# One PSUM bank per projection, 128-wide transposes, a 512-wide half of the down projection, row turns inside gate and up, and fewer waits in a decode block

## The chip, the cores and the metric

The kernel runs on one core of one Trainium2 chip. The metric is the device time of one execution in microseconds (us), lower is better. Before the change the median of three runs is 440.13 us (439.95 to 440.18).

Five engines of the core work side by side and meet only through semaphores: TensorE (PE, matrix products and transposes, writing to the accumulation memory PSUM), VectorE (DVE), ScalarE (ACT), GpSimd (POOL) and SyncE (SP, which here only issues DMAs). Sixteen DMA engines move data between the large memory and the on-chip memory (SBUF).

## The reference

One decoding step of a transformer block for 8 sequences with one new token each: a modulation computed from a condition vector, grouped-query attention over a cache of 8192 positions (32 query heads, 4 key/value heads, head size 128), and a gated feed-forward network with a ReLU gate.

```python
mod = (_silu(c) @ w_mod).reshape(8, 6, 1, -1)            # c: 8 x 1024, w_mod: 1024 x 6144
sa, ca, ga, sb, cb, gb = (mod[:, i] for i in range(6))
h = _layernorm(x) * (1 + ca) + sa                         # x: 8 x 1 x 1024
q = h @ wq                                                # wq: 1024 x 4096, 32 heads of 128
scores = einsum(q, k) * Dh ** -0.5                        # k: 8 x 4 x 8192 x 128
o = einsum(softmax(scores), v) @ wo                       # wo: 4096 x 1024
x = x + ga * o
h = _layernorm(x) * (1 + cb) + sb
gate, up = h @ W_gate, h @ W_up                           # 1024 x 3584 each
x = x + gb * ((relu(gate) * up) @ W_down)                 # W_down: 3584 x 1024
```

Everything is bfloat16; the two caches hold 134 MB, the weights 51 MB. Each byte is read once.

## The kernel before, in words

**The stream.** All large inputs go through one SBUF buffer, `ring`, of five slots of 4 MB (`A_` to `E_`). `stream` lists the loads in the order in which SP issues them: wq in two halves, w_mod in two halves, the key block of the first pair, and then key block n+1 and value block n in turn; the two halves of wo; gate, up, gate, up in halves; W_down as `wd` 0 to 4 (half of it, a quarter, and the last quarter in pieces of four, two and one seventh). A pair n (of 16) is one sequence with two of its four key/value heads: 4 MB of keys, 4 MB of values. Each load waits until the last PE instruction that read the slot's former content is done, so SP's queue is held back by PE alone (L697 to L703).

**The graph.** `_Graph` records operations per engine with the operations that each depends on. `number` gives each engine a counting semaphore and `waits` turns dependencies into waits, leaving out those that the same engine has already waited for. The 16 pairs are emitted as a loop over two pairs (`emit`, L123 to L166): the instructions of the body are stored once and run eight times, and a wait inside it costs a register addition ahead of it.

**Head.** c and x are loaded as rows (8 x 1024), silu is applied to c, and both are turned to columns by PE transposes. `layernorm(xT)` is prepared. When a half of w_mod lands, 48 products of 8 columns of `siluT` with 512 columns of w_mod go to three PSUM banks: output j lies in bank j, in four strips of 32 partitions of which 8 are used. Three copies, twelve f32 transposes and three more copies give `modT`. wq is handled in the same way in two banks. `to_rows` turns the last modulation (gb) to rows, in 32 small f32 products.

**Pairs.** A pair takes 16 steps j (L609 to L647). In each, `slot_keys` transposes 1024 key vectors on PE (8 transposes of 128x128 into one of three PSUM banks), and DVE (even j) or ACT (odd j) copies the bank to `KT`. `slot_scores` multiplies them with the query. Amid the steps of pair n stands the softmax of pair n-1: maximum (`soft_max` to `soft_nb`, j = 2 to 5), exponentials and their sums on ACT (`soft_exp`, j = 6, 128 partitions x 1024), turning P to columns (`turn_p`, j = 8: 32 transposes of 64x64 into two banks, then two copies on DVE and two on ACT), and the product with the values (`pv`, j = 9 to 15). `early` puts the waits of `turn_p` on the last key transpose ahead of it.

**Tail.** `wo_part`, residual and `layernorm(x1T)`, `to_rows` of x1, then gate and up (128 products), ReLU and product, seven transposes to `hmT`, and the down projection: 112 products of 256 columns into bank `W`, four strips of 32 partitions. Two DVE operations add the residual and four small DMAs write the output.

## Time and profile before

| what | value |
|---|---|
| time, median of three runs | 440.13 us |
| time of the profiled execution | 440.24 us |
| its span, first to last instruction | 438.2 us |
| bytes read | 185.63 MB, 424 GB/s over the span |
| busy: PE, weight loads, DVE, ACT, POOL | 306.2, 198.5, 176.8, 187.4, 11.2 us |
| instructions executed | 11766 |
| DMA queue q1 (the stream): packets, share of 16 engines | 6928, 98.4% |
| DMA queue q8 (instructions): packets, MB | 10, 0.16 |
| last weights land, output DMAs issued | 434.5, 435.9 us |

Times in views of the trace are microseconds from the start of the span; the 2.0 us by which the execution is longer than its span lie outside it. Busy times can overlap, so a large one alone says nothing about what the time hangs on; the chain of waits and the tables by stage do.

### The profile page before, as it was taken

How to read it: one execution, taken by the hardware profiler on the slowest of the kernel's cores; microseconds unless marked ns; L12 is line 12 of the kernel's file. 1: busy time of each engine (PE TensorE's matmuls, PEld its weight loads, DVE VectorE, ACT ScalarE, POOL GpSimd, SP SyncE). 2: the span in 40 equal slices, each digit the busy share in tenths (PEclk: the TensorE clock that was granted, in tenths of full speed). 3: DMA queues.
4: the chain of work that ended last, by engine and by line, in shares of the span. 5: the costliest groups of instructions: out<-in, count | busy, mean ns of one | idle time of the engine just before them, and what ended most of it. 6: DMA issues, size and time to landing. Idle time of an engine off the chain costs nothing.

```text
span 438.2 us, 11766 instructions
## 1 busy us (share of the span) xinstructions
PE 306.2 (70%) x4987; PEld 198.5 (45%) x4987; DVE 176.8 (40%) x377; ACT 187.4 (43%) x214; POOL 11.2 (3%) x49
## 2 busy tenths in 40 slices
PE   0104267989888888788887878878888878565053
PEld 0101035656555655555555555555555655331031
DVE  4200046456363554535364444536355455330010
ACT  3000015566654746564574646547465655300000
POOL 4000000000000000000000000000000000000000
PEclk9999599999999999998999989999899999965586
DMA  8999999999999999999999999999999999999994
GB/s 350 446 449 449 413 432 424 428 432 427 431 431 431 431 431 434 434 431 434 434 434 440 440 437 434 431 434 434 431 431 431 431 431 431 436 436 420 428 428 181
DMA packets 7004, 185.83 MB, mean 424 GB/s; under 512 B 800, under 2 KB 832, under 8 KB 1104
## 3 DMA queue, kind: packets, MB, share of 16 engines
q1 hardware_dynamic: 6928, 185.61, 98.4%
q8 instruction: 10, 0.16, 0.1%
q10 hardware_dynamic: 64, 0.04, 0.0%
q14 instruction: 2, 0.02, 0.0%
HBM read 185.63 MB, written 0.02 MB: 424 GB/s over the span
## 4 chain that ended last, share of the span: by engine, by line
DMA 59%; PE 26%; DVE 6%; issue 5%; ACT 2%; SPq 1%; DVEq 0%; ACTq 0%
DMA ring<-in_A_k_cache_dram 34%; PE PS L374 14%; PE PS L370 12%; DMA ring<-in_w_mod_dram 11%; DMA ring<-in_B_W_down_dram 7%; DMA ring<-in_B_W_up_dram 7%; DVE KT L378 3%; ACT KT L381 2%; DVE tm L378 1%; SPq L700 1%; DVE nm L378 1%; ACT P L381 0%; DVE nb L378 0%; DVE qT L378 0%; DVE rl L378 0%
## 5 line engine op out<-in xcount | busy, mean ns | idle before, releaser
L381 ACT ACTIVATE KT<-PS 128x1024 bf16<-128x1024 bf16 (+1 forms) x132 | 132.8, 1008 | 164.5 <-PE PS L374 79.9
L374 PE MATMUL PS<-identb,ring 128*128 128x128 bf16 x2048 | 159.8, 223 | 34.7 <-DMA ring<-in_A_k_cache_dram 21.3
L378 DVE COPY KT<-PS 128x1024 bf16<-128x1024 bf16 (+1 forms) x130 | 89.6, 690 | 178.3 <-PE PS L374 117.9
L374 PEld LDWEIGHTS PS<-identb,ring 128*128 128x128 bf16 x2048 | 120.5, 100 | 79.4 <-issue 46.2
L370 PE MATMUL PS<-KT,Z 128*32 128x512 bf16 x516 | 54.3, 396 | 0.2 <-ACT KT L381 0.2
L370 PE MATMUL PS<-ring,pt 128*32 128x256 bf16 x1088 | 50.0, 275 | 0.8 <-DVE pt L378 0.8
L370 PE MATMUL PS<-ring,siluT 128*8 128x512 bf16 x96 | 9.6, 576 | 31.5 <-DMA ring<-in_w_mod_dram 31.5
L370 PEld LDWEIGHTS PS<-ring,pt 128*32 128x32 bf16 x1088 | 23.0, 95 | 13.2 <-issue 0.9
L381 ACT ACTIVATE pt<-PS 64x512 bf16<-64x512 bf16 x34 | 20.1, 591 | 16.7 <-PE PS L374 16.3
L381 ACT ACT_TABLE_LOAD x11 | 14.1, 1283 | 24.0 <-PE PS L374 22.3
L370 PE MATMUL PS<-ring,h2T 128*8 128x512 bf16 (+1 forms) x128 | 11.2, 519 | 15.9 <-DMA ring<-in_B_W_up_dram 11.0
L381 ACT ACTIVATE P<-PS,nb 128x1024 bf16<-128x1024 f32 x17 | 18.9, 1113 | 6.5 <-DVE nb L378 5.6
L370 PEld LDWEIGHTS PS<-KT,Z 128*32 128x32 bf16 x516 | 13.8, 93 | 15.3 <-ACT KT L381 1.7
L378 DVE TENSOR_REDUCE mp<-PS 128x1 f32<-128x1024 f32 x17 | 20.7, 1215 | 0.0
L370 PEld LDWEIGHTS PS<-ring,siluT 128*8 128x8 bf16 x96 | 2.9, 115 | 37.9 <-DMA ring<-in_w_mod_dram 32.3
L378 DVE COPY pt<-PS 64x512 bf16<-64x512 bf16 x34 | 14.2, 417 | 2.7 <-PE PS L374 2.1
L370 PEld LDWEIGHTS PS<-ring,h2T 128*8 128x8 bf16 x128 | 3.6, 113 | 23.0 <-DMA ring<-in_B_W_up_dram 12.6
L370 PE MATMUL PS<-od,selo 128*128 128x128 f32 x36 | 9.8, 359 | 5.0 <-DVE od L378 5.0
L378 DVE TENSOR_TENSOR KT<-PS,KT 128x512 bf16<-128x512 f32 (+1 forms) x2 | 1.2, 619 | 26.4 <-ACT KT L381 26.4
L374 PE MATMUL PS<-identb,KT 8*128 8x8 bf16 (+1 forms) x31 | 2.5, 211 | 13.2 <-DMA KT<-in_A_x_dram 8.2
L374 PE MATMUL PS<-identb,P 64*64 64x64 bf16 x544 | 11.8, 194 | 0.0
L598 POOL CAST ot<-og 128x16 bf16<-128x16 f32 x16 | 4.1, 255 | 287.2 <-DVE og L378 287.2
(88 smaller groups left out, 158.4 us busy)
## 6 DMA issues: line engine op xcount, KB each, us to landing
ring<-in_A_k_cache_dram SPq DMA_DIRECT2D x16, 4096.0 KB, 21.1
ring<-in_A_v_cache_dram SPq DMA_DIRECT2D x16, 4096.0 KB, 30.0
ring<-in_w_mod_dram SPq DMA_DIRECT2D x2, 6144.0 KB, 42.4
ring<-in_A_wq_dram SPq DMA_DIRECT2D x2, 4096.0 KB, 16.8
ring<-in_A_wo_dram SPq DMA_DIRECT2D x2, 4096.0 KB, 29.4
ring<-in_B_W_gate_dram SPq DMA_DIRECT2D x2, 3584.0 KB, 26.7
ring<-in_B_W_up_dram SPq DMA_DIRECT2D x2, 3584.0 KB, 33.1
ring<-in_B_W_down_dram SPq DMA_DIRECT2D x1, 3584.0 KB, 39.5
```

Of the source, the lines that this page charges most:

```text
L370: return pe(lambda e: e.matmul(out_, lhsT, rhs, start=start, stop=stop, skip_group_check=True), reads, writes, block, deps)
L374: return pe(lambda e: e.matmul(out_, in_, ident, start=True, stop=True, is_transpose=True), reads, writes, block)
L378: return g.op("dve", lambda e: getattr(e, name)(*args, **kw), reads, writes)
L381: return g.op("act", lambda e: e.activation(*args, **kw), reads, writes)
L598: pool(lambda e: e.tensor_copy(dst, og[:, n % 2]), reads=[("og", n % 2)], writes=[("ot", n // B)])
L700: o.fn = (lambda e, key=key, src=src, o=o: e.dma_start(place[key], src).then_inc(o.sem, 16))
```

## The change

Seven edits are made together.

- *Fewer waits.* A new pass `thin` drops every dependency that is implied by another one that the operation, or an earlier one on its engine, already waits for. `early` and the field `apart` go.
- *c and x together.* Both are loaded into one tile of 16 rows and turned together by 8 transposes instead of 16; the sigmoid now waits for both.
- *One bank for w_mod and one for wq.* `siluT` is widened to 40 columns and `hT` to 24, with zeros beside the 8 that count. A product takes 24 (or 16) columns, so that output j falls 8j rows down in the strip and adds zeros to the others; all 96 (64) products accumulate in one bank. One copy and four transposes follow where there were three copies and twelve transposes (two and eight for wq).
- *P in blocks of 128.* `soft_exp` becomes two ACT instructions of 64 partitions each, writing the second half 64 columns further on in a `P` of 1088 columns; `turn_p` turns it with 8 transposes of 128x128 per half, 16 instead of 32.
- *`to_rows` with a wide operand.* DVE spreads the source into `wide` (128 x 8 x 128); 8 f32 products with `rest` replace 32. Constants `part`, `rest`, `fold` and a cleared `wide` are made at the start.
- *Its place.* Both calls now stand after k = 3 of gate and up, ahead of the products that wait for the second halves; one stood before the first key block, the other before gate and up.
- *Half of W_down in 512 columns.* The part of `wd` 0 takes 28 products of 512 columns into bank `Y`, a copy to `yR`, and two f32 products with `fold` that put the sum into `W`; the other half goes on in `W` as before.

The built programs hold 1205 PE products before and 1063 after; the program of PE has 2641 instructions before and 2262 after, counting the weight load of each product, and four for an f32 product that is no transpose.

```diff
--- before.py
+++ after.py
...
+    def thin(self):
+        place = {id(o): (eng, i) for eng, ops in self.prog.items() for i, o in enumerate(ops)}
+        name = lambda d: ("dma", id(d.sem)) if d.sem is not None else place[id(d)][0]
+        value = lambda d: d.semval if d.sem is not None else place[id(d)][1] + 1
...
+                    kept = set()
+                    for k, d in best.items():
+                        v = value(d)
+                        if base.get(k, 0) >= v:
+                            continue
+                        if any(known[id(x)].get(k, 0) >= v for y, x in best.items() if y != k):
+                            continue
+                        kept.add(k)
...
     def number(self):
+        self.thin()
...
-        siluT = sb("siluT", [128, KD, B], bf16)
+        siluT = sb("siluT", [128, KD, 5 * B], bf16)
-        hT = sb("hT", [128, KD, B], bf16)
+        hT = sb("hT", [128, KD, 3 * B], bf16)
-        P = sb("P", [128, 1024], bf16)
+        P = sb("P", [128, 1088], bf16)
...
+                        (Z[:], 0.0, ("Z", 0)), (siluT[:], 0.0, "siluT"), (hT[:], 0.0, "hT"), (pt[:], 0.0, "pt"), (od[:], 1.0, "od"), (P[:], 0.0, ("P", 0)), (KT[:, 6, :], 0.0, ("KT", 6)), (KT[:, 7, :], 0.0, ("KT", 7))):
...
+        dve("memset", wide[:], 0.0, writes=["wide"])
+        for i in range(2):
+            dve("tensor_reduce", fold[:, i].rearrange("p (h s r) -> p h s r", h=2, s=2)[:, :, i, :],
+                identf[:].rearrange("p (a h r) -> p h r a", a=2, h=2), AX.X, ALU.add, reads=["identf", "fold"], writes=["fold"])
...
+        g.dma("act", KT[B:2 * B, 0, :], c, csem, 16, writes=["c"])
+        g.dma("act", KT[0:B, 0, :], A_x.rearrange("b o d -> (b o) d"), xsem, 16, writes=["x"])
+        act(sig, row, ACT.Sigmoid, reads=["c", "x"], writes=[("KT", 1)])
...
+        for k in range(KD):
+            tr(TB(0)[:, 2 * B * k:2 * B * (k + 1)], sig[:, k::KD], identb[0:2 * B, 0:2 * B], [("KT", 1), "identb"], [pT[0]])
...
             for j in range(3):
                 for q in range(4):
-                    mm(bank(j)[32 * q:32 * q + B, :], siluT[:, k, :], fourths(w, 2 * j + q // 2, q % 2), k == 0, k == KD - 1,
-                       ["siluT"], [pB[j]], ("mod", k // 4))
+                    mm(bank(0)[32 * q:32 * q + 3 * B, :], siluT[:, k, (2 - j) * B:(5 - j) * B], fourths(w, 2 * j + q // 2, q % 2),
+                       k + j == 0, k == KD - 1 and j == 2, ["siluT"], [pB[0]], ("mod", k // 4))
+        dve("tensor_copy", modR, bank(0), reads=[pB[0]], writes=[("KT", 0)])
+        t = PS[:, 4, :]
+        for i in range(4):
+            tr(t[:, 128 * i:128 * (i + 1)], modR[:, i::4], identf[:], [("KT", 0), "identf"], [pT[0]])
         for j in range(3):
-            if j == 1:
...
-            t = PS[:, 4 + j, :]
-            for i in range(4):
-                tr(t[:, 128 * i:128 * (i + 1)], modR[j][:, i::4], identf[:], [("KT", j), "identf"], [pT[j]])
             dve("tensor_copy", modT[:, 2 * j:2 * j + 2].rearrange("p s (h i) b -> p i (s h) b", h=2),
-                t.rearrange("p (i q x) -> p i q x", i=4, q=4)[:, :, :, 0:B], reads=[pT[j]], writes=["modT"])
+                t.rearrange("p (i q x) -> p i q x", i=4, q=4)[:, :, :, B * j:B * (j + 1)], reads=[pT[0]], writes=["modT"])
...
-                mm(bank(j)[32 * q:32 * q + B, :], hT[:, k, :], w[:, 512 * f:512 * (f + 1)], k == 0, k == KD - 1,
-                   ["hT"], [pB[j]], ("wq", k // 4))
+                mm(bank(1)[32 * q:32 * q + 2 * B, :], hT[:, k, (1 - j) * B:(3 - j) * B], w[:, 512 * f:512 * (f + 1)],
+                   k + j == 0, k == KD - 1 and j == 1, ["hT"], [pB[1]], ("wq", k // 4))
+        dve("tensor_copy", qR, bank(1), reads=[pB[1]], writes=[("KT", 2)])
+        for i in range(4):
+            tr(TB(0)[:, 128 * i:128 * (i + 1)], qR[:, 128 * i:128 * (i + 1)], identb[:], [("KT", 2), "identb"], [pT[0]])
...
         def to_rows(dst, dkey, src, skey):
-            dve("memset", W[:, 0:256], 0.0, writes=[pW])
+            dve("tensor_tensor", out=wide.rearrange("p k (q x) -> p k q x", q=4)[:, :, :, 0:B], in0=src[:, :, None, :].to_broadcast([128, KD, 4, B]),
+                in1=part[:, None, :, None].to_broadcast([128, KD, 4, B]), op=ALU.mult, reads=[skey, "part"], writes=["wide"])
             for k in range(KD):
-                for q in range(4):
-                    mm(W[32 * q:32 * q + B, 32 * k:32 * (k + 1)], src[:, k, :], identf[:, 32 * q:32 * (q + 1)], True, True, [skey, "identf"], [pW])
+                mm(W[:, 32 * k:32 * (k + 1)], wide[:, k, :], rest[:], True, True, ["wide", "rest"], [pW])
             dve("tensor_copy", dst.rearrange("p (x k) -> p k x", k=8), W[:, 0:256].rearrange("p (k x) -> p k x", k=8), reads=[pW], writes=[dkey])
-
-        to_rows(gbR[:], "gbR", modT[:, 5], "modT")
...
         def soft_exp(n):
-            act(P[:], S(n).rearrange("p h c -> p (h c)"), ACT.Exp,
-                bias=nb[:], scale=SCALE, accum_out=od[:, 128:129], reads=[pS(n, 0), pS(n, 1), "nb"], writes=["P", "od1"])
-
+            for gl in range(2):
+                r = slice(64 * gl, 64 * (gl + 1))
+                act(P[r, 64 * gl:64 * gl + 1024], S(n)[r].rearrange("p h c -> p (h c)"), ACT.Exp,
+                    bias=nb[r], scale=SCALE, accum_out=od[r, 128:129], reads=[pS(n, 0), pS(n, 1), "nb"], writes=[("P", gl), ("od1", gl)])
         def turn_p(n, h):
             t = t_bank()
-            at = len(g.prog["pe"])
             for i in range(8):
-                for gl in range(2):
-                    r = slice(64 * gl, 64 * (gl + 1))
-                    tr(TB(t)[r, 64 * i:64 * (i + 1)], P[r, 512 * h + 64 * i:512 * h + 64 * (i + 1)], identb[r, r], ["P", "identb"], [pT[t]])
-            if n + 1 < NP:
-                early(at)
-
+                at = 64 * (8 * h + i)
+                tr(TB(t)[:, 128 * i:128 * (i + 1)], P[:, at:at + 128], identb[:], [("P", 0), ("P", 1), "identb"], [pT[t]])
...
-        modulate(h2T, "h2T", 3, 4)
-        to_rows(x1R[:], "x1R", x1T, "x1T")
+        modulate(h2T[:], "h2T", 3, 4)
...
+            if k == 3:
+                to_rows(gbR[:], "gbR", modT[:, 5], "modT")
+                to_rows(x1R[:], "x1R", x1T[:], "x1T")
...
-        for c_ in range(4):
+        for t in range(14):
+            w = place[("wd", 0)][:, t // 7, t % 7, :]
+            for h in range(2):
+                at = 64 * (t % 2) + 32 * h
+                mm(Y[at:at + B, :], hmT[:, t % 7, t // 7, :], w[:, 512 * h:512 * (h + 1)], t < 2, t >= 12, ["hmT"], [pY], ("wd", 0))
+        dve("tensor_copy", yR[:], Y, reads=[pY], writes=["yR"])
+        for i in range(2):
+            mm(W[:, 0:256], fold[:, i], yR[:, 256 * i:256 * (i + 1)], i == 0, False, ["yR", "fold"], [pW])
+        for c_ in (2, 3):
             for i in range(7):
-                if c_ < 2:
-                    key, w = ("wd", 0), place[("wd", 0)][:, c_, i, :]
-                elif c_ == 2:
+                if c_ == 2:
...
                 for q in range(4):
-                    mm(W[32 * q:32 * q + B, 0:256], hmT[:, i, c_, :], w[:, 256 * q:256 * (q + 1)], c_ + i == 0, c_ == 3 and i == 6,
+                    mm(W[32 * q:32 * q + B, 0:256], hmT[:, i, c_, :], w[:, 256 * q:256 * (q + 1)], False, c_ == 3 and i == 6,
                        ["hmT"], [pW], key)
```

## The prediction

> **What bounds the kernel now.** I read the page from the DMA row to the chain of waits, then the last microseconds in tables by stage, then one pair in order of time.

> ```profile
> DMA  8999999999999999999999999999999999999994
> GB/s 350 446 449 449 413 432 424 428 432 427 431 431 431 431 431 434 434 431 434 434 434 440 440 437 434 431 434 434 431 431 431 431 431 431 436 436 420 428 428 181
> ...
> q1 hardware_dynamic: 6928, 185.61, 98.4%
> q8 instruction: 10, 0.16, 0.1%
> ...
> DMA 59%; PE 26%; DVE 6%; issue 5%; ACT 2%; SPq 1%; DVEq 0%; ACTq 0%
> ```

> The sixteen DMA engines are never idle between the first and the last slice: the kernel is its stream. PE's 26% in the chain are the steps at which a slot comes free, and a load that is issued then stands behind others: the key load issued at 253.42 us lands at 275.60, 22 us for 4 MB that take 9.7 us at 432 GB/s. Nothing that PE, DVE or ACT do faster amid the stream can shorten it; only its start, its end, and what the DMA engines carry besides can.

> The end, in windows of 1 us; the last two columns are the DMA engines' share and GB/s:

> ```profile
> 430.00:431.00 1.00, 0.97 (x28) 0.59 (x28) 0.00 (x0) 0.00 (x0) 0.00 (x0) 0.85 0.94 369
> 431.00:432.00 1.00, 0.09 (x4) 0.00 (x0) 0.00 (x0) 0.00 (x0) 0.00 (x0) 0.50 0.63 254
> 432.00:433.00 1.00, 0.28 (x8) 0.21 (x12) 0.00 (x0) 0.00 (x0) 0.00 (x0) 0.50 0.30 119
> 433.00:434.00 1.00, 0.80 (x20) 0.23 (x16) 0.00 (x0) 0.00 (x0) 0.00 (x0) 0.50 0.13 51
> ```

> The share falls over three microseconds: the engines do not finish together, and the last two (0.13 of 16) decide when the weights are there. The chain ends on that:

> ```profile
> 405.17 28.73 DMA ring<-in_B_W_down_dram
> 433.90 0.04 issue
> 433.95 0.60 PE PS L370 x7
> 434.55 0.02 issue
> 434.56 0.41 PE PS L370 x4
> 434.98 0.02 issue
> 435.00 0.44 DVE ov L378
> ```

> **Why two engines are late.** The trace holds every DMA packet with queue, start, duration and size. On a busy engine a packet starts 3 to 4 ns before its predecessor ends, which separates the sixteen series; all carry the same sequence of sizes. Their last weight packets end so: six engines at 430.8 to 431.1 us; two, which took an 8 KB packet of another instruction queue (at 76.3 and 101.9), at 431.9; six, which took one 16 KB packet of q8, at 432.3 to 432.5; two, which took two of those, at 433.87 and 434.01. So one q8 packet sets its engine back by about 1.4 us (0.95 for itself, 0.45 for a slower packet after it; at 430.72 an 8 KB packet takes 787 ns instead of 309), and an engine that is never idle never makes it up.

> The ten come at 55.7, 70.4, 77.2, 85.8, 93.1, 100.5, 377.6, 387.4, 403.7 and 429.8 us: none in the last seven passes of the loop. 16 KB are 256 instructions of 64 bytes, and PE's program has 2641, so eleven blocks, ten after the first. Along PE's program each packet comes some 80 instructions ahead of a multiple of 256, 3 to 4.4 us late. The first eight hit eight different engines; the ninth hits that of the first, the tenth that of the second.

> [...]

> **The change, part by part.**

> *Head.* Three more memsets on POOL stand ahead of `identf` (by `pt`, 1.82 us for 2048 columns, some 1.4 us for their 1600), and DVE gets some 3 us of constants (four reductions of 0.2 to 0.4, a 1024-column clear bounded by the 0.53 of 512 columns twice). The sigmoid now waits for x, which lands at 8.16, not for c alone (2.98). Together siluT and the layer norm, ready at 12.8 and 16.3, come 5 to 8 us later; w_mod lands at 37.12. Cost 0; without that cover, up to 8 us.

> *w_mod and wq.* The same 96 and 64 products. Wider weights are bounded by 0.115 (8 columns) and 0.093 us (32 columns) a load, both beside the products; accumulating in one bank has no row: bounded below by 0 and above by doubling the second batch of 4.61 us. After it two copies, eight f32 transposes (0.14 each) and, for wq, four of bf16 fall away: about 0.6 us; `to_rows` of gb (1.2 us) goes. PE starts on the keys 1.5 to 2 us sooner than 67.28. This buys nothing: the keys of pair 0 have landed before, and key block 1, value block 0 and wo, issued at 56.62 and 63.36, keep the engines busy past 90. At the upper bound the first of them slips to 61.2, where the sixteen engines end the keys of pair 0 (60.3 to 61.9): up to 0.9 us of idle. I take 0, since the four strips that run side by side are as before.

> *Pairs.* From the pair at 275.60:

> ```profile
> 282.26 1.11 ACT L381 ACTIVATE P<-PS,nb 128x1024 bf16<-128x1024 f32 x1
> ...
> 283.37 1.01 ACT L381 ACTIVATE KT<-PS 128x1024 bf16<-128x1024 bf16 x1
> 284.43 0.10 PEld L374 LDWEIGHTS PS<-identb,ring 128*128 128x128 bf16 x1 [0.75 <-ACT KT L381]
> ...
> 284.60 0.69 PE L374 MATMUL PS<-identb,P 64*64 64x64 bf16 x32
> ...
> 292.16 0.33 SPq L700 DMA_DIRECT2D ring<-in_A_k_cache_dram  x1
> ```

> The second ACT half is unseen: bounds 0.59 (the 64x512 copy to `pt`) and 1.11 us (128x1024 exponential), plus 0.19 for the sum; I take 1.11 as the nearer in columns, so ACT +1.3. The j = 7 copy behind it on ACT, for whose bank the second half of `turn_p` waits, slips by as much. The first half starts at about 284.6, the second at 285.7, and both cost 8 x 128x128 (0.62, the key rows) where 32 small ones took 0.69. The next key step slips from 285.54 to 286.4, so the pair from 16.6 to some 17.7 us. What falls away in waits I count at nothing. The stream gives 19.4 us per pair (issues at 253.42, 274.15 and 292.16), so PE waits shorter for the next keys. Cost 0; bounds 0 and 15 times what a pair takes beyond 19.4.

> *Gate, up and the turns.* gate and up first halves wait for up at 399.04; h2T is ready at 393.43. The two `to_rows` now run from 403.7 on PE: 8 f32 products each, bounded by 0.25 us (the `pick` rows: 2.04 for four) and 0.5 us each, 4 to 8 us with two DVE copies of 0.63 and two spreads of 0.4 to 1.0. Behind them waits only the first gate product of the second half (landed 408.86), which in any case waits on with its followers for up at 417.33. Cost 0, and SP's next load waits for the last gate product ahead of them (404.05), unmoved.

> *Down.* 28 products of 512 columns for 56 of 256: wo's 32 of that form took 1.99 us, so 1.74 against 1.70. Then 0.69 for the copy and two f32 products of 256 columns, 1.0 to 1.9 us (128 columns: 0.5). `wd` 0 lands at 425.79, so `W` is ready at 429.3 to 430.2, and `wd` 1 lands at 430.03; its 1.06 us have until 432.72. Cost 0; without that cover up to 0.8 us, when the clock is at half, as it is in the last window.

> *Instruction blocks.* PE's program shrinks to 2262: 8.8 blocks, eight after the first. By the order above they hit eight different engines, and the last weight packet ends at 432.5 instead of 434.0: -1.5 us. The last four products (0.41), two DVE steps and the output DMAs follow as before. A block ahead of need for instruction 2304 would be asked for near 2224, among the products of `wd` 2, which PE can't pass before about 431.2; 3 us on, the stream is over.

> Sum: 440.24 (profiled execution) - 1.5 = 438.7 us. The median of the runs is 0.1 below that execution, which I leave in the range. 0.2% (0.9 us) is about what a measurement can tell from no change.

> **Rivals.** *No gain, 440.2.* Fetches may stop mattering for the end, or two of the eight may share an engine: the choice of engine is read from ten cases only. The slowest of the two late engines then ends where it did. For it speaks that the loop's five fetches cost PE nothing visible; against it, that lateness and packets match on all sixteen engines. [...]

> *Half a gain, 439.3 to 439.9.* A ninth block is asked for earlier, or the copy and `fold` run at the half clock and PE is 0.6 to 0.8 us behind the last load.

> *Slower, 443.* If the split exponential and the blocks of 128 make a pair longer than the stream's 19.4 us, PE falls behind in each. At the end 5.6 us (393.4 to 399.0) and 4.4 us (after the turns, to the last up block, near 416: 417.33 less the second hit of 403.7) are spare, 10 in all over 15 pairs: it decides from 20.0 us a pair, 3.4 more than now, where I find 1.1. At 20.3 the lag is 14 us, 4 beyond the spare: 440.2 - 1.5 + 4.2 = 442.9.

> **Numbers.** Forecast 0.62, no gain 0.18, half a gain 0.12 (split over the bound), slower 0.08. The forecast's own range is 438.2 to 439.1: ends of engines with one packet differ by 0.3, its delay by 0.3. The range runs from there to 440.4, past the case of no gain, and leaves out 0.1 above. Faster 0.69, same 0.22, slower 0.09.

> **What would show it.** q8 with 8 packets (9 with one after 433 us); the last weights at PE near 433.0 instead of 434.56; DMA rows at 9 throughout; the key loads still some 19.4 us apart; DVE waiting less for `wd`. Wrong: a last landing at 434.5 with eight q8 packets, an idle DMA engine amid the pairs, or PE busy when the last load lands.

## The result and the profile after

The kernel after takes 438.55 us (median of seven runs, 438.53 to 438.86) where the kernel before takes 440.13 (439.95 to 440.20) beside it: a ratio of 0.9966, 95% interval 0.9956 to 0.9976, so 1.58 us or 0.36% faster. The forecast was 438.7 with a range of 438.2 to 440.4. The profiled execution is one of 438.55 us with a span of 436.6.

The page of the kernel after, its DMA row, two of its queues and the shares of the chain of work that ended last:

```profile
DMA  8999999999999999999999999999999999999995
...
q1 hardware_dynamic: 6928, 185.61, 98.7%
q8 instruction: 9, 0.15, 0.1%
...
DMA 54%; PE 23%; issue 8%; DVE 8%; ACT 6%; SPq 1%; DVEq 0%; ACTq 0%
```

The stream carries the same 6928 packets and is as dense as before (9 in every slice between the first and the last), and the same bytes are done sooner. The end, first in windows of 1 us (columns: window, its length, busy time of PE, PEld, DVE, ACT and POOL, granted clock, DMA share, GB/s), then as the chain:

```profile
431.00:432.00 1.00, 0.61 (x16) 0.30 (x16) 0.00 (x0) 0.00 (x0) 0.00 (x0) 1.00 0.67 266
432.00:433.00 1.00, 0.40 (x10) 0.11 (x10) 0.00 (x0) 0.00 (x0) 0.00 (x0) 0.99 0.33 119
433.00:434.00 1.00, 0.38 (x4) 0.09 (x4) 0.54 (x2) 0.00 (x0) 0.00 (x0) 0.50 0.00 0
```

```profile
404.40 28.55 DMA ring<-in_B_W_down_dram
432.95 0.04 issue
433.00 0.41 PE PS L422 x3
433.41 0.02 issue
433.43 0.43 DVE ov L430
433.87 0.02 issue
433.89 0.42 DVE outR L430
```

Between 433 and 434 us the DMA share is 0.00, where it was 0.13 before: the two engines that came last are gone. The last weights reach PE at 433.00 instead of 434.56, and from there the same steps of 0.41, 0.43 and 0.42 us follow. The whole gain in the span (438.2 to 436.6) lies in that landing, and all the down weights show it: `wd` 0 is at PE at 424.50 (before 425.79), `wd` 1 at 428.73 (430.03), `wd` 2 at 431.16 (432.72).

The packets say why. Their times, here and in the prediction, count from 0.13 us after the start of the span, so they read 0.13 us lower than the views. The nine of q8 come at 55.6, 75.1, 84.8, 93.1, 102.7, 378.7, 388.5, 419.8 and 432.3 us. The first eight are on eight different DMA engines; the ninth starts within 5 ns of the end of its engine's last weights. Six engines end at 430.9 to 431.2, two with an 8 KB packet at 431.7 and 432.1, and eight with one 16 KB packet at 432.3 to 432.5. None ends later.

### The profile page after: what moved, and what is told of

Read it like the earlier page. It is cut to its first block, busy times and chain, and to the rows that moved or that the text cites. A ratio compares the mean times of both kernels' runs of the same rounds, so it can differ in the third digit from the quotient of the medians.

```text
span 436.6 us, 10734 instructions
## 1 busy us (share of the span) xinstructions
PE 306.9 (70%) x4575; PEld 199.4 (46%) x4575; DVE 180.0 (41%) x384; ACT 208.6 (48%) x246; POOL 12.7 (3%) x52
## 3 DMA queue, kind: packets, MB, share of 16 engines
q1 hardware_dynamic: 6928, 185.61, 98.7%
## 4 chain that ended last, share of the span: by engine, by line
DMA 54%; PE 23%; issue 8%; DVE 8%; ACT 6%; SPq 1%; DVEq 0%; ACTq 0%
DMA ring<-in_A_k_cache_dram 29%; PE PS L426 12%; DMA ring<-in_w_mod_dram 11%; PE PS L422 11%; DMA ring<-in_B_W_down_dram 7%; DMA ring<-in_B_W_up_dram 6%; ACT P L433 3%; DVE KT L430 2%; ACT KT L433 2%; DVE tm L430 1%; DVE ov L430 1%; DVE nm L430 1%; SPq L747 1%; DVE nb L430 0%; DVE rl L430 0%
## 5 line engine op out<-in xcount | busy, mean ns | idle before, releaser
L426 PE MATMUL PS<-identb,ring 128*128 128x128 bf16 x2048 | 152.8, 220 | 19.3 <-DMA ring<-in_A_k_cache_dram 17.6
L426 PEld LDWEIGHTS PS<-identb,ring 128*128 128x128 bf16 x2048 | 117.0, 98 | 58.5 <-issue 37.3
L422 PE MATMUL PS<-KT,Z 128*32 128x512 bf16 x516 | 51.9, 390 | 0.1
L433 ACT ACTIVATE P<-PS,nb 64x1024 bf16<-64x1024 f32 x34 | 37.7, 1109 | 6.2 <-DVE nb L430 4.2
L426 PE MATMUL PS<-identb,P 128*128 128x128 bf16 x272 | 21.0, 221 | 20.2 <-ACT P L433 14.5
L422 PEld LDWEIGHTS PS<-ring,pt 128*32 128x32 bf16 x1088 | 24.5, 95 | 12.8 <-issue 0.8
L422 PE MATMUL PS<-ring,siluT 128*24 128x512 bf16 x96 | 9.8, 584 | 27.5 <-DMA ring<-in_w_mod_dram 27.5
L426 PEld LDWEIGHTS PS<-identb,P 128*128 128x128 bf16 x272 | 15.3, 98 | 26.5 <-DVE KT L430 17.2
L433 ACT ACTIVATE pt<-PS 64x512 bf16<-64x512 bf16 x34 | 20.1, 592 | 13.5 <-PE PS L426 13.2
L430 DVE COPY pt<-PS 64x512 bf16<-64x512 bf16 x34 | 14.4, 422 | 17.7 <-PE PS L426 17.2
L422 PEld LDWEIGHTS PS<-ring,siluT 128*24 128x24 bf16 x96 | 3.1, 125 | 33.5 <-DMA ring<-in_w_mod_dram 28.3
L426 PE MATMUL PS<-identb,KT 128*128 128x128 bf16 (+1 forms) x19 | 1.7, 218 | 18.4 <-DVE KT L430 18.4
```

What stands on the lines that cost most here:

```text
L422: return pe(lambda e: e.matmul(out_, lhsT, rhs, start=start, stop=stop, skip_group_check=True), reads, writes, block, deps)
L426: return pe(lambda e: e.matmul(out_, in_, ident, start=True, stop=True, is_transpose=True), reads, writes, block)
L430: return g.op("dve", lambda e: getattr(e, name)(*args, **kw), reads, writes)
L433: return g.op("act", lambda e: e.activation(*args, **kw), reads, writes)
```

## The experiments

Four questions were open: whether it is the instruction packets, whether any other edit has a part in the gain, what order the packets follow, and how thin the cover is under which the longer pairs cost nothing.

### One block more in the kernel after

```diff
+        def filler(n):
+            for i in range(n):
+                q = 32 * (i % 4)
+                mm(PS[q:q + B, 5, 0:32], identf[:, 0:B], identf[:, q:q + 32], True, True, ["identf"], [pT[1]])
...
         layernorm(xT, "xT")
+        filler(64)
```

> The kernel after, with 64 small f32 products (four PE instructions each) that write to a bank that is overwritten later, put into the head just ahead of the first products with w_mod, where PE waits for w_mod anyway: PE's program grows from 2262 to 2518 instructions, one block of 256 more. Theory (instruction packets set a DMA engine back): the packets come one block earlier along the program, the ninth now near 414 us, amid the stream, on the engine that took the first; the tenth near the end, harmless. That engine's last weight packet ends near 433.9, time 440.0. Rival (the gain came from the other edits, fewer waits and shorter stages): 438.6, unchanged.

Measured: 440.12 us, ratio to before 1.0003 (0.9993 to 1.0012). Sixty-four tiny products in a stretch in which PE only waits (they run from 19.45 to 21.35 us, and the first products with w_mod wait for it until 38.46) give the whole gain back. One of the eleven executions took 442.31, the others 439.80 to 440.26; it was not traced. The page, and the chain's end:

```profile
q8 instruction: 10, 0.16, 0.1%
```

```profile
425.96 3.19 PE PS L422 x28
...
429.92 5.16 PE PS L422 x46
435.08 0.02 issue
435.10 0.43 DVE ov L430
```

The ninth packet comes at 419.7 and one engine now ends at 433.99 (its last eight packets stand 0.08 us apart from 433.43 on, alone); the others end by 432.84. `wd` 0 is at PE at 425.96 instead of 424.50. This execution also shows a forecast rival at work, PE at half clock (0.50 from 430 to 434): its products run from 425.96 with no break but the copy to `yR`, and end at 435.08, 0.1 us after those of the kernel before. By these rows the 9.1 us from `wd` 0's landing to the last product would have ended at 433.6 in the kernel after, 0.2 beyond what it did. So the half clock is worth 0.2 us there at most; the rest is the late landing.

### One and two blocks less in the kernel before

```diff
         def to_rows(dst, dkey, src, skey):
-            dve("memset", W[:, 0:256], 0.0, writes=[pW])
-            for k in range(KD):
...
+            dve("memset", dst, 0.0, writes=[dkey])
```

> The kernel before without the two turnings to rows: the rows of gb and of x1 are set to zero instead, so the residual and the gate of the second half are left out. PE's program goes from 2641 to 2387 instructions, one block less. Theory: nine packets; the ninth still comes amid the stream and hits the engine of the first, so one engine keeps two hits and the time stays near 440.0 to 440.1, though PE has 64 products less. Rival (each instruction or each product saved is worth its share of 1.6 us over 379 instructions): about 439.0.

```diff
-        for c_ in range(4):
+        for c_ in (2, 3):
```

> The kernel before without the two turnings to rows (their rows are zero) and without the products with the first half of W_down (its weights are loaded as before, but not multiplied): PE's program has 2275 instructions, two blocks fewer than before and 13 more than after. Theory: eight packets that matter, on eight different engines, so 438.6, as the kernel after, although none of its other edits is made. Rival (the gain comes from the shorter stages, the fewer waits or the new order): 440.1.

Measured: 440.08 us with one block less, ratio 0.9999 (0.9990 to 1.0008), and 438.88 with two, ratio 0.9973 (0.9963 to 0.9982). The page and chain of the first:

```profile
q8 instruction: 9, 0.15, 0.1%
```

```profile
404.85 29.07 DMA ring<-in_B_W_down_dram
433.91 0.04 issue
433.96 0.60 PE PS L370 x8
```

And the chain of the second:

```profile
404.92 27.49 DMA ring<-in_B_W_down_dram
432.41 0.04 issue
432.45 0.60 PE PS L370 x7
```

Both pages count nine q8 packets. In the first the ninth comes at 428.3, amid the stream, and one engine ends at 434.05. In the second it comes at 432.5, behind the stream, and the last engine ends at 432.58. A cut of 254 instructions, 64 products among them, is worth nothing while the ninth packet stays; moving that one packet behind the stream is worth 1.2 us. The second has none of the change's edits, and keeps four fifths of its gain. Of the 0.3 us by which it is behind the kernel after, 0.1 lies in the span (436.7 against 436.6) and 0.2 outside it.

### The pass that drops waits, alone

```diff
     def number(self):
+        self.thin()
```

> The kernel before with the pass that drops implied waits, and nothing else: 2636 PE instructions, ten blocks after the first as before. Theory: ten packets, two engines hit twice, 440.1. Rival (the waits and the register additions that they cost inside the loop slow the pairs or the issuing of loads): less than 440.1, down to 438.6 if they were the whole gain.

Measured: 440.25 us, ratio 1.0003 (0.9994 to 1.0012), with ten q8 packets and two engines ending last, at 433.85 and 433.92. The pass does nothing for the time by itself.

### One block less in the kernel after

```diff
-            for i in range(16):
+            for i in range(2 if gp == 0 else 16):
...
-        for k in range(KD):
+        for k in (0, 1, 2, 3, 7):
...
-        for t in range(14):
+        for t in (12, 13):
```

> The kernel after with 264 PE instructions less, one block: the two turnings to rows (rows zero), the gate and up products of k = 4, 5 and 6, the products with the first half of wo but for two of 16, and those with the first half of W_down but for two of 14 are left out; all weights are loaded as before. Theory: seven or eight packets that matter, each on an engine of its own, so that the last engine still has one hit: 438.55, nothing gained. Rival (each block less is worth 1.5 us): 437.0.

Measured: 438.74 us, ratio 0.9972 (0.9964 to 0.9981). Seven packets instead of nine, the last engine at 432.61 instead of 432.53, no gain. Eight of the eleven executions lie at 438.58 to 438.86, the others at 439.54 to 440.18; the profiled one, 439.54, has a span of 436.7, as in the kernel after. Together with the others:

| kernel | PE instructions | q8 packets ahead of the end | last weight packet ends, us | time, us |
|---|---|---|---|---|
| after, one block less | 1998 | 7 | 432.61 | 438.74 |
| after | 2262 | 8 | 432.53 | 438.55 |
| before, two blocks less | 2275 | 8 | 432.58 | 438.88 |
| before, one block less | 2387 | 9 | 434.05 | 440.08 |
| after, one block more | 2518 | 9 | 433.99 | 440.12 |
| before with `thin` | 2636 | 10 | 433.92 | 440.25 |
| before | 2641 | 10 | 434.01 | 440.13 |

It is a step between eight packets and nine, with nothing on either side of it. The engines follow the packets one by one: with seven, seven engines end between 432.2 and 432.9 and none later; with eight, eight and none; with nine, seven there and one near 434.0; with ten, six there and two near 434.0. The others have ended by 432.1 in all seven traces.

### Eight and nine blocks more

```diff
+        filler(128)
         for k in range(KD):
             tr(TB(0)[:, 2 * B * k:2 * B * (k + 1)], sig[:, k::KD], identb[0:2 * B, 0:2 * B], [("KT", 1), "identb"], [pT[0]])
...
         layernorm(xT, "xT")
+        filler(256)
...
         for k in range(KD):
+            if k == 4:
+                filler(128)
```

The second has 320 where this has 256.

> The kernel after with 512 of the same small products in three places of the head: 2048 PE instructions more, eight blocks. Theory: seventeen packets, sixteen of them in time to matter, so that each of the eight engines is hit twice and none three times, the last harmless: the end is again that of an engine with two hits, 440.0, the same as with one block more. Rival A (the cost is in the number of instructions that PE goes through, or in bytes): eight times what one block costs, about 449 to 450. Rival B (nothing to do with it): 438.6.

> The kernel after with 576 of the same small products: 2304 PE instructions more, nine blocks. Theory: seventeen packets in time to matter, so that one engine is hit three times and its last weight packet ends near 435.3: 441.4, a step of 1.4 above the run with eight blocks more. If the cost went by the number of instructions, the step between the two would be an eighth of what eight blocks cost; if packets don't matter, 438.6 for both.

Measured: 445.43 and 448.41 us, 5.4 and 7.0 more than expected. Neither theory holds, for a reason that the windows of the first show:

```profile
25.00:30.00 5.00, 1.89 (x128) 1.74 (x128) 0.00 (x0) 0.00 (x0) 0.00 (x0) 0.50 1.08 465
30.00:35.00 5.00, 0.00 (x0) 0.00 (x0) 0.00 (x0) 0.00 (x0) 0.00 (x0) 0.50 1.08 465
35.00:40.00 5.00, 1.89 (x128) 1.74 (x128) 0.00 (x0) 0.00 (x0) 0.00 (x0) 0.50 0.89 383
...
60.00:65.00 5.00, 3.87 (x46) 1.59 (x36) 0.09 (x1) 0.00 (x0) 0.00 (x0) 0.81 0.21 88
```

PE goes through one block (64 f32 products, counted here as 128 products and 128 weight loads) and then stands still until after the next packet has come (17.3 us between 20 and 45 us, up to 5.6 at a time); the packets are 5.7 to 8.5 us apart (12.4, 18.4, 25.6, 32.6, 40.0, 47.1, 55.6, 61.3). The products with w_mod come late, the slots come free late, and between 60 and 65 us the DMA engines are at 0.21: the stream has run dry. Summed over the packets, the sixteen engines carry no load of the stream for 4.9 us more than in the kernel after up to 430 us (0.5 of it are the eight more instruction packets, the rest is idle), and the packets of the stream themselves take 2.0 us more per engine (32 KB packets of up to 2.3 us instead of 1.21 around the dry stretch): 6.9 of the 7.4 us by which this profiled execution (445.94) is longer. For the other the same sum gives 6.6 and 2.3, 8.9 of 9.9.

If a stream that runs dry brings all engines level again, what was late before it no longer counts; no run shows that by itself. Both kernels have eight packets between the dry stretch and the end, and in both the last engine ends within half a microsecond of the next ones, as with one packet each; but in the second, four engines end at 442.1 to 442.5, a microsecond behind the other twelve, which is not explained. The question of the order of the engines was thus not put by these two runs.

### Four blocks more, where PE waits

```diff
         layernorm(xT, "xT")
+        filler(128)
...
+            if k == 4:
+                filler(64)
...
                 to_rows(x1R[:], "x1R", x1T[:], "x1T")
+                filler(64)
```

> The kernel after with 256 of the small f32 products, put where PE waits longest: 128 behind the layer norm of x, 64 between the halves of w_mod, 64 behind the turning to rows: 1024 PE instructions, four blocks more, spread so that the stream of loads should not run dry (with eight and nine blocks more in the head it stood idle for 4 to 6 us). Theory (each packet sets back the next of eight engines in turn): twelve packets matter, four engines have two hits, none three: 440.1, as with one block more. Rival (each block costs its 1.5 us wherever it lands): 438.55 + 4 x 1.57 = 444.8.

Measured: 440.19 us (median of 12), ratio 1.0005 (0.9996 to 1.0015), where a cost for each block would have given 444.8. Ten of the twelve executions lie at 439.97 to 440.41. The other two, the profiled one among them, took 442.2 and 442.6. In that one the stream was dry for 0.6 us more, and one engine ended 1.2 us after the next (436.26 and 435.03), which would fit a third packet on one engine. So the median shows that twelve packets cost no more than nine. On which engines they fell in those ten executions was not traced, and that the turn through eight engines is always kept is not shown.

### How much longer a pair may take

The forecast let a pair grow to 20.0 us before it would cost anything. Extra exponentials on ACT, written to a tile that nobody reads, lengthen it:

```diff
         def soft_exp(n):
+            for i in range(2):
+                r = slice(64 * (i % 2), 64 * (i % 2) + 64)
+                act(extra[r, :], S(n)[r].rearrange("p h c -> p (h c)"), ACT.Exp, bias=nb[r], scale=SCALE,
+                    reads=[pS(n, 0), pS(n, 1), "nb", ("extra", i % 2)], writes=[("extra", i % 2)])
```

> The kernel after with two more exponentials of 64 x 1024 per pair on ACT, written to a tile that nothing reads: 2.2 us more per pair ahead of the second half of the turn of P, so about 19.9 us per pair where PE doesn't wait for the stream. The forecast's slack (10 us over 15 pairs, from 20.0 us a pair) gives 438.6, at most 439.5. Rival (no slack behind the pairs, every pair beyond the stream's 19.4 us moves the end): 438.6 + 15 x 0.55 = about 447.

> The kernel after with three more exponentials of 64 x 1024 per pair on ACT, 3.3 us per pair, about 21.0 us per pair. The forecast's slack is used up: 438.6 + 15 x (21.0 - 19.4) - 10 = about 453. Rival (work on ACT and PE amid the pairs is hidden whatever it takes): 438.6. Rival (no slack): about 463.

Measured: 471.19 and 486.91 us. The pairs took 21.3 and 22.5 us (mean distance of the key loads' issues from 88.5 to 365.7 and from 87.4 to 380.1), more than the 2.2 and 3.3 us that were added to 17.7 (at a mean granted clock of 0.885 and 0.873, where the kernel after has 0.945), and the slack of 10 us isn't there. With the sum of idle and slower packets again: 20.3 and 10.5 us per engine in the first, 30.8 of its 31.0; 36.6 and 10.6 in the second, all of its 47.2. So the time is lost where the stream runs dry amid the pairs, and what PE has to spare behind them did not bring it back. Without slack, 438.6 + 15 x (pair - 19.36) gives 468.0 and 486.0; the profiled executions, from which the pairs are, took 469.5 and 485.7.

With one extra exponential (`range(1)`):

> The kernel after with one more exponential of 64 x 1024 per pair on ACT (1.1 us). With two and three more the PE-bound pairs took 21.3 and 22.5 us; with one they should take between 19.4 and 20.1. The forecast's slack of 10 us gives 438.6 up to 20.0 us a pair. Theory formed after the two slower kernels (no slack: the last loads wait for PE as well, so each pair beyond the stream's 19.36 us moves the end): 438.6 + 15 x (pair - 19.36), so 443.6 at 19.7 and 449.7 at 20.1.

Measured: 447.73 us (445.56 to 449.34), ratio 1.0173 (1.0152 to 1.0195). The profiled execution is the shortest, 445.56; its pairs take 19.95 us in the mean, so that the theory without slack gives 438.6 + 15 x 0.59 = 447.4, 1.9 too much for it, and the forecast's slack 438.6, 7.0 too little. Idle time (2.2) and slower packets (4.7) make up 6.9 of these 7.0 us. The pairs are not alike, though. Three in a row, from one key load's issue to the next:

```profile
264.38:284.56 20.18, 17.22 (x252) 11.51 (x252) 9.47 (x19) 14.05 (x16) 0.34 (x2) 0.92 1.00 430
284.56:303.29 18.73, 15.77 (x252) 10.79 (x252) 9.48 (x19) 12.77 (x15) 0.34 (x2) 1.00 0.98 402
303.29:323.26 19.97, 17.15 (x252) 11.64 (x252) 9.47 (x19) 14.05 (x16) 0.34 (x2) 0.91 0.99 425
```

The middle one, at full clock, is 18.73 us: 1.0 more than the 17.73 of the kernel after, and under the stream's 19.36. Eleven of the 13 pairs have the lower clock and take 20.0 to 20.3. Inside the last one, PE's operations (start, duration, and in brackets the idle time before them), then windows of 1 us:

```profile
311.47 0.62 PE L427 MATMUL PS<-identb,ring 128*128 128x128 bf16 x8
313.99 0.76 PE L427 MATMUL PS<-identb,P 128*128 128x128 bf16 x8 [1.90 <-ACT P L434]
314.96 1.03 PE L427 MATMUL PS<-identb,P 128*128 128x128 bf16 x8 [0.21 <-ACT KT L434]
315.79 1.06 PE L427 MATMUL PS<-identb,ring 128*128 128x128 bf16 x8
```

```profile
313.00:314.00 1.00, 0.01 (x1) 0.02 (x2) 0.00 (x0) 0.98 (x3) 0.00 (x0) 1.00 0.91 393
...
315.00:316.00 1.00, 1.00 (x10) 1.00 (x11) 0.63 (x2) 0.00 (x0) 0.00 (x0) 0.50 0.91 393
316.00:317.00 1.00, 1.00 (x12) 0.72 (x14) 0.00 (x0) 0.96 (x2) 0.00 (x0) 0.50 1.07 459
317.00:318.00 1.00, 1.00 (x17) 0.41 (x10) 0.00 (x0) 0.97 (x2) 0.00 (x0) 0.63 1.06 459
```

Whether the clock is the cause was tested by giving PE something to do in that gap:

```diff
             t = t_bank()
+            if h == 0:
+                for i in range(16):
+                    tr(TB(t)[:, 128 * (i % 8):128 * (i % 8 + 1)], identb[:], identb[:], ["identb"], [pT[t]])
```

> The kernel with one more exponential per pair (447.7), in which PE waits 1.9 us for the second half of P and the clock of TensorE is granted at 0.91 over most pairs, and 16 transposes of the identity more, put ahead of the first half of the turn of P, where PE waits anyway (they write to the bank that the turn then overwrites; 2358 PE instructions). Theory (the pair is 18.7 us at full clock, under the stream's 19.36, and the loss is the lower clock that follows the longer wait): with PE busy in the wait the clock is 1.00, the pairs take 18.7 to 19.4 us, and the time is 438.6, or up to 440.1 where the ninth instruction packet, 96 instructions earlier along the program, still hits a busy DMA engine. Rival (the clock has nothing to do with that wait): clock 0.91 and 447 to 448 as without them.

Measured: 440.03 us, ratio 0.9996 (0.9986 to 1.0005). Sixteen useless transposes per pair take 7.7 us off. Two stretches of its pairs, and the end of its chain:

```profile
140.00:160.00 20.00, 17.93 (x292) 12.37 (x284) 10.15 (x20) 14.46 (x17) 0.34 (x2) 1.00 1.01 436
200.00:220.00 20.00, 17.93 (x286) 12.63 (x284) 10.37 (x21) 14.03 (x17) 0.34 (x2) 1.00 0.99 429
```

```profile
405.18 29.33 DMA ring<-in_B_W_down_dram
434.51 0.04 issue
434.55 0.41 PE PS L423 x4
```

The clock is 1.00, the PE-bound pairs take 18.73 us each, and later ones follow the stream at 19.35 to 19.38. What is left above 438.55 is the ninth packet: it now comes at 428.3, and one engine ends at 434.03.

## Why the prediction was right, step by step

**The stream as the bound: right.** Work was taken from PE (`b_cut1`'s turnings to rows) or given to it (one block more) at no effect of its own, and the losses in the traces are late engines, or a dry stream with the slow packets around it.

**1.4 us for a packet, never made up: right.** The step between eight packets and nine is 1.2 to 1.6 us in the time, and 1.4 to 1.5 in the last weight packet, in kernels that share nothing else of the change. The term of -1.5 was measured as -1.56 at the landing.

**Eight engines in turn: right for the ninth and tenth packet**, which is all the sum needed. Beyond that the median with twelve fits and one execution does not.

**The packet for instruction 2304: right that it costs nothing, off by 0.7 us in its place** (432.3 instead of behind 433), and so without the margin that the forecast saw. By the views' clock it starts at 432.46, 1.3 us after the products of `wd` 2 could begin and not 3, just as its engine ends its weights; in `b_cut2` it does so as well. Whether it had been waiting behind them, or would have cost 1.4 us a little sooner, is not shown.

**Head: cost 0, right; its lateness smaller.** `siluT` and the layer norm came 4.4 us later (16.96 and 20.52), not 5 to 8.

**w_mod and wq: cost 0, right; the saving did not come.** PE was to start on the keys 1.5 to 2 us sooner than 67.28; it started at 68.50, and the first pair freed its key slot at 85.65 instead of 84.27. The second w_mod batch took 5.30 us (4.61 before) and the wq batch 5.32 (3.63). In both the clock was granted at about half (0.50 from 62 to 64, where the kernel before has 1.00). That one bank is to blame isn't shown: the kernel with one block more has the same banks, the clock at 1.00 between 60 and 65, a wq batch of 3.63, and freed its slot at 84.36. Its PE started on the keys at 67.22, so even at full clock the saving is not there.

**Pairs: cost 0, right; the size right by luck, the growth too large, and the margin wrong.** Where PE sets the pace the key loads are issued at 85.65, 103.39, 121.12 and 138.85, so a pair takes 17.73 us, the 17.7 of the forecast. But two errors cancel in it. The kernel before takes 17.3 us there (84.27, 101.49, 118.79): the 16.6 of the forecast run from the first product with the landed keys to the next key load (275.60 to 292.16) and leave out some 0.7 us of a pair. And the pair grew by 0.5 and not by 1.1: in the forecast's own measure it now takes 17.07 (275.54 to 292.61). The pair in which the forecast followed the two ACT halves and the two turns:

```profile
282.01 1.11 ACT L433 ACTIVATE P<-PS,nb 64x1024 bf16<-64x1024 f32 x1
...
283.24 1.11 ACT L433 ACTIVATE P<-PS,nb 64x1024 bf16<-64x1024 f32 x1
...
284.57 0.62 PE L426 MATMUL PS<-identb,P 128*128 128x128 bf16 x8 [0.91 <-ACT P L433]
...
285.55 0.62 PE L426 MATMUL PS<-identb,P 128*128 128x128 bf16 x8 [0.36 <-ACT KT L433]
```

The 1.11 us and the starts of the turns came as worked out. What stands around them was smaller: the exponentials start 0.2 us sooner behind the first key product (6.47 us against 6.66), a saving in waits that the forecast counted at nothing, and the next key step follows at 286.00 and not 286.4. What failed is the condition of the rival "slower, 443": that 10 us behind the pairs are spare, so that it decides from 20.0 us a pair. At 19.95 the loss was 7.0 us in that execution. PE's spare time at the end is waiting for loads, and a PE that is late in the pairs issues those loads late too (the first of gate at 383.95 with one extra exponential, at 370.05 without). It decides from the stream's 19.36. That rival deserved a dearer price and a nearer point, though the change stays 1.6 us per pair short of it at full clock.

**Turns to rows: right.** Each took 1.97 us of products (4 to 8 with the rest were forecast; the second ended at 408.2), the first gate products behind them ran right then, and those that follow waited for up until 415.88.

**Down: right.** The copy took 0.69, `fold` 1.13 us, and `W` was ready at 428.1, earlier than forecast because `wd` 0 was there earlier, 0.6 before `wd` 1. The clock was at 1.00 there; in the kernel with one block more it was at half, and `W` was ready only at 432.0, so the cover that the forecast counted on is thin.

**No gain (440.2)** went by fetches that stop mattering for the end. For PE they don't matter in the kernels before and after: on their chains no "issue" ahead of a piece of PE is longer than 0.17 and 0.23 us. For the DMA engine that carries the block they do, by 1.4 us. And in the run with eight blocks more, where 256 instructions of PE fall within 5 us (1.89 of them busy), they matter for PE too: it then stands still for up to 5.6 us.

## What to carry to other kernels

When a stream keeps all DMA engines busy from start to end, look at how far apart they finish: here each 16 KB packet with code of the busiest engine that came amid the stream made one of them late for good, by about 1.4 us, and only the latest counted (434.01 us before, 432.53 after). Count the blocks of instructions ahead of the end; a shorter program paid here only where it took the last double hit away (440.08 us with nine packets ahead of the end, 438.88 with eight), and a block less on either side of that step paid nothing (440.08 against 440.13, 438.74 against 438.55). And measure the cover of a "free" delay in the steady state: here 1.1 us more on ACT for each of 16 pairs cost 9 us, through the clock (0.91 over most pairs), although the pair at full clock, 18.73 us, would still have fitted under the stream's 19.36.

## What was not expected of the hardware

- With one extra exponential a gap of 1.9 us in PE's work, where 0.9 us in the kernel after had no effect (clock 1.00 in its pairs), was followed by 3.4 us at half clock in most pairs: wherever it left PE busy for at most 1.51 us of one 3.41 us step of the clock; sixteen dummy transposes in the gap kept the clock at 1.00 and took the time from 447.73 to 440.03 us.
- Beside the stream (DMA share 0.89 to 1.08 from 20 to 40 us) the blocks of straight PE code came 5.7 to 8.5 us apart (16 KB for 256 instructions, so 64 bytes each, in the run with eight blocks more), and PE went no faster through short products.
- When the stream ran dry, the packets around the gap were slow as well: 10.5 us per engine of longer packets beside 20.3 us of idle time with two extra exponentials. Why they are slow was not examined.
